# List scatters behind the state decays and two weight splits a step later in attention; expert 2's rows transposed during expert 1's first GEMM

## The chip, the cores and the metric

One NeuronCore of a Trainium2 chip runs the whole program. The metric is the device time of one execution in microseconds, the median of several runs. Five engines work side by side, each through its own instruction stream in order: TensorE (PE, matrix products; its weight loads are PEld), VectorE (DVE), ScalarE (ACT), GpSimd (POOL) and SyncE (SP, which here does nothing but issue transfers). They wait for each other through semaphores. POOL also issues the indirect transfers (gathers and scatters by a list of row numbers).

## The reference

Two stages. The first is linear attention with decay for 4 batches, 8 heads, 768 positions of 64 numbers, in blocks of 64; the second is a mixture of 8 experts of which each of the 3072 tokens takes 2.

```python
# attention, block b of 64 positions
intra = np.einsum('bhic,bhjc->bhij', qb, kb) * Dmask[None]
intra = np.einsum('bhij,bhjd->bhid', intra, vb)
inter = np.einsum('bhid,bhde->bhie', qb * lam_pow[None], kv_state)
out[:, :, sl] = intra + inter
kv_state = lam_block[None, :, None, None] * kv_state + np.einsum('bhsd,bhse->bhde', kb_dec, vb)
...
# experts; x is the attention output, 3072 x 512
noisy_logits = x @ w_gate + np.log1p(np.exp(x @ w_noise)) * noise
top2 = np.argpartition(-noisy_logits, 2, axis=1)[:, :2]        # and softmax of the two
for e in range(E):
    for k in range(2):
        mask = top2[:, k] == e
        h = np.maximum(x[mask] @ w1[e], 0.0)                   # 512 x 1024
        out[mask] += top2_w[mask, k, None] * (h @ w2[e])       # 1024 x 512
```

## The kernel before

**Attention.** Twelve steps t = 0 to 11 of 256 positions each (two chunks of 128, all heads). A step transposes keys and queries of the next step (`trans_k`, `trans_q`), updates the states (`kv`), forms the output (`intra`, `inter`, evacuated by `evac_o` on ACT as `xo`), transposes the output of the step before to tokens (`turn_x`, ACT tile `xc`, stored as `x_tok`) and computes its gate logits. In `kv`, POOL multiplies a state by its decay (line 408, "S") and DVE adds the new product (line 409). The gate's many small DVE instructions are generators that `advance(n)` lets run a few at a time between the steps; `gate`, `route` and `weights` make for each token its two experts, its place in their lists and its weights.

**Lists.** Each chunk of 128 tokens and each of the two choices is one indirect transfer of POOL (`scatter_list`, line 622) that writes 128 records to the lists `lst` in DRAM: 48 of them. `paced(n, tile)` puts a one-element POOL copy in front of n of them, so that they start no earlier than the tile that it reads.

**Weights.** All products of the experts run in three passes with a high and a low part of each fp32 operand. A weight tile is loaded to a staging tile `wst` (four buffers), ACT makes the high part (line 768) and POOL or DVE the low part (line 772). During attention the tables `LOADS`, `HIGH`, `LOW` give the step in which each of expert 0's tiles is loaded and split; `(2, 0)` is the first tile of its second weight.

**Experts.** Expert 0 runs first, then 1, then 2 to 7 in an order by load. A row of an expert is a token; rows come in tiles of 128, at most 7, the last a shorter one. Per expert: gather the rows of `x_tok` (`gather_rows`, POOL, line 810, tile `xg`), transpose them, split into high and low (`xth`, `xtl`), first GEMM (`gemm1`, 8 blocks f of 128 columns, for each of two parts of the rows; ACT and DVE evacuate, lines 863 and 867), second GEMM (`gemm2`, tile by tile; DVE line 907 adds the earlier output, POOL line 914 scatters it). For experts 2 to 7 the transposition goes through DRAM: `turn_rows` transposes 32 x 32 blocks on DVE into a tile `ot` and SP stores it (lines 829 and 831), `fetch_rows` reads it back on SP in four transfers (line 836), `split_rows` makes the two parts on ACT and DVE (lines 843 and 844). The tiles `ot` are three buffers, shared by `turn_rows` and the results of `gemm2`.

For experts 3 to 7, `turn_rows` and `fetch_rows` stand in the second part of the first GEMM of the expert before, and only `split_rows` in its second GEMM. For expert 2 they all stand between the tiles of expert 1's second GEMM (lines 1169 to 1176): after `gemm2(1, t)` the split of weight tile t, the load of the next weight tile, the fetch of row tile t - 1, the turning of row tile t, and the split of row tile t - 1. The last tile (`late`) is split in expert 2's first GEMM. The order is the order of the code: nothing rearranges it.

Of the kernel before, what the change touches and what calls it, by code (L numbers as in the profile page):

```python
# [39 lines left out]
FB = F // 128  # L40
# [21 lines left out]
HIGH = {4: [(1, 0)], 5: [(1, 1)], 6: [(1, 2)], 7: [(1, 3)], 8: [(2, 0)], 9: [(2, 1)]}  # L62
# [21 lines left out]
def size(e, t):  # L84
    return TS if t < NT - 1 else TAILS[e]
# [31 lines left out]
def kernel(  # L117
# [174 lines left out]
    def scatter(n):  # L292
        for job in scatters[:n]:
            scatter_list(*job)
        del scatters[:n]
# [125 lines left out]
    XC = {}  # L421
# [243 lines left out]
    def paced(n, tile):  # L665
        if scatters:
            nc.gpsimd.tensor_copy(spacer, tile[0:1, 0:1])
            scatter(n)
# [265 lines left out]
    for t in range(NST):  # L934
        u = t + 1
        if t:
            products(t - 1)
            turn_x(t - 1)
            paced(1, XC[t - 1][:, 1, 0, :])
# [6 lines left out]
        if u < NST:  # L946
            kv(u)
        kdecay(t + 2)
        scatter(1)
# [8 lines left out]
        paced(1, XO[t][:, 1, 0, :])  # L958
# [12 lines left out]
        if u < NST:  # L971
            if LOW.get(t):
                nc.gpsimd.tensor_copy(spacer, AT[u][0][0:1, 0, 0, 0, 0:1])
            for which, j in LOW.get(t, []):
                split_low(which, 0, j, low=nc.gpsimd)
# [151 lines left out]

    for e in range(1, E):
# [4 lines left out]
        for i, (t0, n) in enumerate(parts(e)):  # L1133
            for f in range(FB):
# [8 lines left out]
                if e == 2 and not i and f == 1:  # L1143
                    split_rows(late, size(2, late))
                    gather_rows(3, late)
# [15 lines left out]
        for t in range(tiles(e)):  # L1161
            gemm2(e, t)
            if e == 1:
                next(ovj, None)
            if e + 1 < E:
                if t < 4:
                    split_w(1, e + 1, t)
                    load_w(2, e + 1, t)
                for j in nxt[t - 1:t] if e == 1 and t else ():
                    fetch_rows(j, size(2, j))  # L1170
                for j in nxt[t:t + 1] if e == 1 else ():
                    turn_rows(j, size(2, j))
                for j in (nxt[t - 1:t] if t else ()) if e == 1 else nxt[t:t + 1]:
                    split_rows(j, size(e + 1, j))
                    if e + 2 < E and j < tiles(e + 2):
                        gather_rows(e + 2, j)
        if e == 1:
            late = nxt[-1]
            fetch_rows(late, size(2, late))
# [62 lines left out]
```

## Time and profile before

| | |
|---|---|
| median of 3 runs (lowest, highest) | 738.89 us (736.31, 739.82) |
| profiled execution, its own time | 741.05 us |
| its span, first to last instruction | 739.3 us |
| busy PE, PEld | 706.7 us (96%), 601.7 us (81%) |
| busy DVE, POOL, ACT | 357.6 us, 274.9 us, 237.0 us |
| mean granted clock of TensorE | 0.989 |

The profile's rows give a start and a duration in microseconds, the engine, the line of the kernel, and for each group what the engine waited for. PE is the engine that is almost always busy, so what matters is where it stands still. "The chain" is the work that ended last, followed back step by step to what released it.

### The profile page before, as it was taken

What the parts mean: (1) busy time and instruction counts of PE and PEld (TensorE: products, weight loads), DVE (VectorE), ACT (ScalarE), POOL (GpSimd) and SP (SyncE); (2) the same over time, 40 slices, a digit from 0 to 9 for tenths busy, and PEclk for the clock granted to TensorE, in tenths of its full rate; (3) what the DMA queues carried; (4) which work ended last, traced back from release to release, by engine and by line L of the source; (5) the groups of instructions that cost most, each with busy time, mean ns of one, the idle gap of its engine ahead of it and who ended that gap; (6) DMA issues with size and microseconds to landing.
All of it is one profiled execution on the core that took longest, in us unless ns stands there. A gap on an engine that the chain in (4) does not pass through costs nothing.

```text
span 739.3 us, 13508 instructions
## 1 busy us (share of the span) xinstructions
PE 706.7 (96%) x4917; PEld 601.7 (81%) x4917; DVE 357.6 (48%) x815; ACT 237.0 (32%) x451; POOL 274.9 (37%) x439
## 2 busy tenths in 40 slices
PE   8899998899999999769999999999999999999996
PEld 6788886699888887658888887988798898889885
DVE  6335869777235543455436433644353544335211
ACT  1567685331133320142214221423042322224200
POOL 3200336677756442323252415242512433221311
PEclk9999999999999999989999999999999999999999
DMA  7999997981527636457464636564655556550211
GB/s 162 204 230 232 245 255 210 272 243 39 114 62 264 185 87 195 141 156 217 147 222 138 178 129 228 158 187 145 208 150 178 193 173 180 161 166 14 79 43 38
DMA packets 139594, 122.50 MB, mean 166 GB/s; under 512 B 88554, under 2 KB 107370, under 8 KB 139524
## 3 DMA queue, kind: packets, MB, share of 16 engines
q1 hardware_dynamic: 124996, 85.22, 43.7%
q0 software_dynamic: 13104, 36.34, 15.6%
q8 instruction: 40, 0.66, 0.4%
q14 instruction: 30, 0.25, 0.1%
q10 hardware_dynamic: 1424, 0.04, 0.1%
HBM read 87.15 MB, written 35.55 MB: 166 GB/s over the span
## 4 chain that ended last, share of the span: by engine, by line
PE 75%; DMA 9%; issue 6%; DVE 4%; ACT 2%; SPq 2%; POOL 1%; POOLq 0%; ACTq 0%; DVEq 0%
PE pS L857 34%; PE pKV L895 14%; PE pO L895 12%; DMA wst<-in_moe_w_dram 3%; DMA xg<-turned 2%; PE pS L356 2%; PE pKV L369 2%; PE pO L369 2%; PE pO L900 1%; PE pS L326 1%; PE pS L429 1%; SPq L836 1%; PE pS L401 1%; POOL out_dram L914 1%; DMA qt<-in_q_dram 1%
## 5 line engine op out<-in xcount | busy, mean ns | idle before, releaser
L857 PE MATMUL pS<-xth,w1h 128*128 128x512 f32 (+3 forms) x544 | 182.0, 335 | 7.7 <-DVE ht L867 5.8
L857 PE MATMUL pS<-xtl,w1h 128*128 128x512 f32 (+3 forms) x544 | 181.3, 333 | 0.4 <-DVE xtl L822 0.4
L857 PE MATMUL pS<-xth,w1l 128*128 128x512 f32 (+3 forms) x544 | 181.1, 333 | 0.0
L863 ACT ACTIVATE ht<-pS 128x512 fp32r<-128x512 f32 (+3 forms) x136 | 65.6, 483 | 218.7 <-PE pS L857 213.0
L867 DVE SCALAR_TENSOR_TENSOR ht<-pS,ht 128x256 fp32r<-128x256 f32 (+3 forms) x176 | 76.5, 455 | 112.1 <-ACT ht L863 110.1
L895 PE MATMUL pO<-w2h,ht 128*128 128x512 f32 x384 | 124.1, 394 | 3.9 <-DVE ot L907 3.9
L895 PE MATMUL pKV<-w2h,ht 128*128 128x512 f32 x384 | 123.0, 391 | 0.0
L857 PEld LDWEIGHTS pS<-xth,w1h 128*128 128x128 f32 x544 | 103.5, 190 | 17.6 <-ACT ht L863 6.0
L857 PEld LDWEIGHTS pS<-xtl,w1h 128*128 128x128 f32 x544 | 103.5, 190 | 9.4 <-DVE xtl L822 0.7
L857 PEld LDWEIGHTS pS<-xth,w1l 128*128 128x128 f32 x544 | 103.5, 190 | 8.9
L914 POOL DMA_INDIRECT out_dram<-ot,rec x46 | 59.2, 1286 | 118.3 <-DVE ot L907 110.3
L895 PEld LDWEIGHTS pO<-w2h,ht 128*128 128x128 f32 x384 | 72.8, 190 | 20.7 <-DVE ot L907 4.3
L895 PEld LDWEIGHTS pKV<-w2h,ht 128*128 128x128 f32 x384 | 72.1, 188 | 16.2
L810 POOL DMA_INDIRECT xg<-x_tok,rec x46 | 49.4, 1074 | 91.3 <-DVE xtl L844 45.5
L895 PE MATMUL pO<-w2l,ht 128*128 128x512 f32 x192 | 76.0, 396 | 0.0
L895 PE MATMUL pKV<-w2l,ht 128*128 128x512 f32 x192 | 75.4, 393 | 0.0
L879 POOL DMA_INDIRECT pv<-out_dram,rec x46 | 47.1, 1023 | 31.7 <-issue 25.2
L843 ACT ACTIVATE xth<-xg 128x512 fp32r<-128x512 f32 (+1 forms) x39 | 22.4, 598 | 105.5 <-DMA xg<-turned 105.5
L622 POOL DMA_INDIRECT lst<-recs,dest x48 | 47.7, 993 | 13.6 <-issue 9.0
L844 DVE TENSOR_TENSOR xtl<-xg,xth 128x512 fp32r<-128x512 f32 (+1 forms) x39 | 25.6, 656 | 46.7 <-ACT xth L843 46.7
L1151 POOL COPY spacer<-ht 1x1 f32<-1x1 f32 x53 | 9.4, 177 | 99.6 <-ACT ht L863 99.5
L907 DVE SCALAR_TENSOR_TENSOR ot<-pKV,rec,pv 128x512 f32<-128x512 f32 x21 | 15.8, 750 | 59.8 <-PE pKV L895 57.1
(228 smaller groups left out, 932.3 us busy)
## 6 DMA issues: line engine op xcount, KB each, us to landing
wst<-in_moe_w_dram SPq DMA_DIRECT2D x48, 512.0 KB, 4.6
turned<-ot SPq DMA_DIRECT2D x36, 256.0 KB, 3.1
xg<-turned SPq DMA_DIRECT2D x144, 64.0 KB, 2.1
wst<-in_moe_w_dram SPq DMA_DIRECT2D x32, 256.0 KB, 4.0
kt<-in_k_dram SPq DMA_DIRECT2D x24, 256.0 KB, 5.2
qt<-in_q_dram SPq DMA_DIRECT2D x24, 256.0 KB, 5.5
vt<-in_v_dram SPq DMA_DIRECT2D x24, 256.0 KB, 5.3
x_tok<-xc SPq DMA_DIRECT2D x12, 512.0 KB, 5.4
```

Source lines behind the costliest of these rows:

```text
L369: nc.tensor.matmul(PO[u][a][half(g), hp, :], lhs, rhs, start=n == 1, stop=n == (8 if u % NW or a else 4))
L622: st = nc.gpsimd.indirect_dma_start(out=lst, out_offset=bass.IndirectOffsetOnAxis(ap=r["dest"][:, i, c:c + 1], axis=0), in_=r["rec"][:, c, ...
L810: nc.gpsimd.indirect_dma_start(out=XG[t][:size(e, t)], out_offset=None, in_=x_tok[:rows, :], in_offset=bass.IndirectOffsetOnAxis(ap=at, ax ...
L843: nc.scalar.activation(hi, p, AF.Copy)
L844: nc.vector.tensor_tensor(lo, p, hi.bitcast(FT), op=SUB)
L857: nc.tensor.matmul(p, W1[a][d][:, fs], xt(b, cs)[:, d], start=(d == 0 and i == 0), stop=(d == DB - 1 and i == 2))
L863: nc.scalar.activation(ht(e, 0, f, cs), p, AF.Relu)
L867: nc.vector.scalar_tensor_tensor(ht(e, 1, f, c), p[:, r], 0.0, ht(e, 0, f, c).bitcast(FT), op0=OP.max, op1=SUB)
L879: nc.gpsimd.indirect_dma_start(out=PV[t][:size(e, t), :], out_offset=None, in_=out, in_offset=bass.IndirectOffsetOnAxis(ap=REC[e, t][:, 0: ...
L895: nc.tensor.matmul(p, ht(e, a, f, cs), W2[b][f // 2][:, f % 2, :], start=(i == 0), stop=(i == len(terms) - 1))
L907: nc.vector.scalar_tensor_tensor(o, p, w, pv, op0=MULT, op1=ADD)
L914: st = nc.gpsimd.indirect_dma_start(out=out, out_offset=bass.IndirectOffsetOnAxis(ap=REC[e, t][:, 0:1], axis=0), in_=o, in_offset=None, bo ...
```

## The change

Four things. In attention, `paced` after `xc` moves from ahead of the key transposes to behind `kv`, the unpaced `scatter(1)` goes, a scatter paced by the scores' tile `at` comes in ahead of the low split, and the last step's `xo` paces two: three list scatters a step as before, in other places. The high splits `(2, 0)` and `(2, 1)` move from steps 8 and 9 to 9 and 10. For expert 2, `turn_next(k)` turns row tile k and fetches row tile k - 2; it stands in the second part of expert 1's first GEMM from block f = 3 on, and then ahead of each `gemm2(1, t)`. The splits are made one place earlier, and `late` is gone.

```diff
--- before.py
+++ after.py
@@ -59,7 +59,7 @@
 FILLA, FILLB, FILLC = {4: 24, 5: 24, 6: 20, 7: 20, 8: 19, 9: 19, NST - 1: 24}, 2, 4
 FILL1, FILL2 = 4, 9
 LOADS = {2: [(1, 0)], 4: [(1, 1)], 5: [(1, 2)], 6: [(1, 3)], 7: [(2, 0)], 8: [(2, 1)], 10: [(2, 2)], 11: [(2, 3)]}
-HIGH = {4: [(1, 0)], 5: [(1, 1)], 6: [(1, 2)], 7: [(1, 3)], 8: [(2, 0)], 9: [(2, 1)]}
+HIGH = {4: [(1, 0)], 5: [(1, 1)], 6: [(1, 2)], 7: [(1, 3)], 9: [(2, 0)], 10: [(2, 1)]}
 LOW = {5: [(1, 0)], 6: [(1, 1)], 7: [(1, 2)], 8: [(1, 3)], 9: [(2, 0)], 10: [(2, 1)]}
 ZEROS = {10: 8, 11: 8}
 MID = 16
@@ -936,7 +936,6 @@
         if t:
             products(t - 1)
             turn_x(t - 1)
-            paced(1, XC[t - 1][:, 1, 0, :])
         if u < NST:
             trans_k(u)
         load(t + 3, "kt")
@@ -945,8 +944,9 @@
         load(t + 3, "qt")
         if u < NST:
             kv(u)
+        if t:
+            paced(1, XC[t - 1][:, 1, 0, :])
         kdecay(t + 2)
-        scatter(1)
         if u == NST:
             logits(t - 1)
         intra(t)
@@ -955,7 +955,7 @@
             store_x(t - 1)
         inter(t, 0)
         evac_o(t)
-        paced(1, XO[t][:, 1, 0, :])
+        paced(1 if u < NST else 2, XO[t][:, 1, 0, :])
         if t and u < NST:
             logits(t - 1)
         if 2 * t in GB[1:]:
@@ -969,8 +969,9 @@
         for which, j in HIGH.get(t, []):
             split_high(which, 0, j)
         if u < NST:
-            if LOW.get(t):
+            if LOW.get(t) and not scatters:
                 nc.gpsimd.tensor_copy(spacer, AT[u][0][0:1, 0, 0, 0, 0:1])
+            paced(1, AT[u][0][:, 0, 0, 0, :])
             for which, j in LOW.get(t, []):
                 split_low(which, 0, j, low=nc.gpsimd)
         advance(FILLA.get(t, 18))
@@ -1125,6 +1126,16 @@
         for i, _ in enumerate(lists(e)):
             load_rec(e, i)
 
+    LAG = 3
+
+    def turn_next(k):
+
+        js = tile_order(2)
+        for j in js[k - 2:k - 1] if k >= 2 else ():
+            fetch_rows(j, size(2, j))
+        for j in js[k:k + 1]:
+            turn_rows(j, size(2, j))
+
     for e in range(1, E):
         if e == E - 1:
             n_over = nc.values_load(ntot[0:1, 0:1], min_val=0, max_val=MAXOV)
@@ -1140,9 +1151,8 @@
                         fetch_rows(f - 1, size(e + 1, f - 1))
                     if f < tiles(e + 1):
                         turn_rows(f, size(e + 1, f))
-                if e == 2 and not i and f == 1:
-                    split_rows(late, size(2, late))
-                    gather_rows(3, late)
+                if e == 1 and i and f >= LAG:
+                    turn_next(f - LAG)
                 if i == 0 and f % 2 == 0:
                     split_w(2, e, f // 2)
                 if i == 0 and f % 2 and e + 1 < E:
@@ -1159,6 +1169,8 @@
             prepare(e + 2)
         nxt = tile_order(e + 1) if e + 1 < E else []
         for t in range(tiles(e)):
+            if e == 1:
+                turn_next(t + FB - LAG)
             gemm2(e, t)
             if e == 1:
                 next(ovj, None)
@@ -1166,17 +1178,10 @@
                 if t < 4:
                     split_w(1, e + 1, t)
                     load_w(2, e + 1, t)
-                for j in nxt[t - 1:t] if e == 1 and t else ():
-                    fetch_rows(j, size(2, j))
-                for j in nxt[t:t + 1] if e == 1 else ():
-                    turn_rows(j, size(2, j))
-                for j in (nxt[t - 1:t] if t else ()) if e == 1 else nxt[t:t + 1]:
+                for j in nxt[t:t + 1]:
                     split_rows(j, size(e + 1, j))
                     if e + 2 < E and j < tiles(e + 2):
                         gather_rows(e + 2, j)
-        if e == 1:
-            late = nxt[-1]
-            fetch_rows(late, size(2, late))
     with tc.For_i(0, n_over) as it:
         e_r = nc.sync.value_load(tab[0:1, 0, bass.ds(it, 1)], min_val=0, max_val=E - 1)
         row = nc.sync.value_load(tab[0:1, 1, bass.ds(it, 1)], min_val=0, max_val=E * STRIDE - OV)
```

The instructions are the same; their places differ. On POOL, around attention step 9: `S` are the state decays, `xc`, `xo` and `at` the tiles that pace, `lst` the lists, `w1l_336` and `w2l_341` low weight parts.

```order
 L772 TENSOR_TENSOR w1l_336<-wst,w1h_332 128x1024
-L667 COPY spacer<-xc 1x1
-L621 MEMSET spacer 1x1
-L622 DMA lst<-recs,dest 29696x2
 L408 TENSOR_TENSOR S_187<-S_186,QS 128x256
 L408 TENSOR_TENSOR S_188<-S_187,QS 128x256
+L667 COPY spacer<-xc 1x1
 L621 MEMSET spacer 1x1
 L622 DMA lst<-recs,dest 29696x2
```

The two decays come first, and the scatter that was ahead of them is behind them. A little further on, at the end of the step:

```order
-L973 COPY spacer<-at 1x1
+L667 COPY spacer<-at 1x1
+L621 MEMSET spacer 1x1
+L622 DMA lst<-recs,dest 29696x2
 L772 TENSOR_TENSOR w2l_341<-wst,w2h_337 128x1024
+L408 TENSOR_TENSOR S_189<-S_188,QS 128x256
```

One scatter now stands between the copy of `at` and the low part, and the next step's decay directly behind the low part.

SP during expert 1's second GEMM, before (`turned_364` to `366` are the stored row tiles 4, 5, 6, `xg` the fetched ones, `wst` weight loads):

```order
L831 DMA turned_364<-ot 128x512
L748 ISA
L748 DMA wst<-in_moe_w_dram 128x2x512
L836 DMA xg_2430<-turned_364 32x4x128 x4
L831 DMA turned_365<-ot 128x512
L748 ISA
L748 DMA wst<-in_moe_w_dram 128x2x512
L836 DMA xg_2432<-turned_365 32x4x128 x4
L831 DMA turned_366<-ot 32x512
```

And after the change, from the end of expert 1's first GEMM on:

```order
L831 DMA turned_364<-ot 128x512
L831 DMA turned_365<-ot 128x512
L836 DMA xg_2430<-turned_364 32x4x128 x4
L831 DMA turned_366<-ot 32x512
L836 DMA xg_2432<-turned_365 32x4x128 x4
L831 DMA turned_360<-ot 128x512
L836 DMA xg_2434<-turned_366 32x128 x4
L831 DMA turned_361<-ot 128x512
L733 TENSOR_LOAD order
```

Three fetches and five stores now precede the record loads of expert 3 (the group that begins with `order`), and the first weight load comes one more fetch and store after those.

DVE at the start of expert 1's second GEMM, before (`xg_2430` is row tile 4, `w1l` the low weight parts, `ot<-pKV` and `ot<-pO` the evacuation of a tile):

```order
L907 SCALAR_TENSOR_TENSOR ot<-pKV,rec_3186,pv_2424 128x512
L1102 TENSOR_TENSOR ovg<-ovg,tail 1x320
L772 TENSOR_TENSOR w1l_333<-wst,w1h_329 128x1024
L829 STREAM_TRANSPOSE ot<-xg_2430 128x512
L907 SCALAR_TENSOR_TENSOR ot<-pO,rec_3186,pv_2425 128x512
L1104 TENSOR_REDUCE ovt<-ovg 1x40
L772 TENSOR_TENSOR w1l_334<-wst,w1h_330 128x1024
L829 STREAM_TRANSPOSE ot<-xg_2432 128x512
L844 TENSOR_TENSOR xtl_348<-xg_2430,xth_346 128x4x128
```

And after:

```order
L829 STREAM_TRANSPOSE ot<-xg_350 128x512
L829 STREAM_TRANSPOSE ot<-xg_2426 128x512
L907 SCALAR_TENSOR_TENSOR ot<-pKV,rec_3186,pv_2424 128x512
L1103 TENSOR_TENSOR ovg<-ovg,tail 1x320
L772 TENSOR_TENSOR w1l_333<-wst,w1h_329 128x1024
L844 TENSOR_TENSOR xtl_348<-xg_2430,xth_346 128x4x128
L829 STREAM_TRANSPOSE ot<-xg_2428 128x512
L907 SCALAR_TENSOR_TENSOR ot<-pO,rec_3186,pv_2425 128x512
```

The first row tile is split one tile sooner, six of the seven transposes are done before the first evacuation, and the seventh before the second.

## Rows read from the trace of the kernel before

**Rows 1.** Busy time by stretch: length, busy us per engine, clock, DMA share.
```profile
267.00:304.00 37.00, 33.08 (x138) 26.66 (x137) 13.71 (x21) 5.49 (x7) 10.23 (x11) 0.95 0.47 140
304.00:324.00 20.00, 12.56 (x74) 11.03 (x73) 8.77 (x20) 4.45 (x8) 7.03 (x10) 0.91 0.51 160
```

**Rows 2.** Chain that ended last: start, duration, work.
```profile
267.03 5.52 PE pKV L895 x24
...
355.37 5.49 PE pO L895 x24
...
388.33 3.65 PE pO L900 x16
391.98 34.45 PE pS L857 x192
```

**Rows 3.** Timeline of PE, expert 1 to 2, rows after a standstill (in brackets).
```profile
298.43 0.50 PE L895 MATMUL pO<-w2h,ht 128*128 128x512 f32 x1 [3.92 <-DVE ot L907]
...
323.49 0.58 PE L857 MATMUL pS<-xth,w1h 128*128 128x288 f32 x1 [5.79 <-DVE ht L867]
```

**Rows 4.** The chain in expert 1's second GEMM, one tile.
```profile
290.01 0.41 SPq L748
...
291.97 4.21 DMA xg<-turned
296.36 0.64 ACT xth L843
...
299.93 0.41 SPq L748
```

**Rows 5.** Timelines of ACT, POOL, SP and DVE near expert 1's second GEMM.
```profile
260.08 0.44 ACT L863 ACTIVATE ht<-pS 128x320 fp32r<-128x320 f32 x1 [1.32 <-PE pS L857]
...
266.65 1.03 POOL L810 DMA_INDIRECT xg<-x_tok,rec  x1 [0.54 <-issue]
...
280.91 1.87 SPq L836 DMA_DIRECT2D xg<-turned  x4
...
274.78 0.69 DVE L829 STREAM_TRANSPOSE ot<-xg 128x512 f32<-128x512 f32 x1
```

**Rows 6.** Transfers from 250 to 330 us: size, median us to landing.
```profile
turned<-ot SPq DMA_DIRECT2D x6, 256.0 KB, 3.5
...
xg<-x_tok,rec POOLq DMA_INDIRECT x14, 3.5
```

**Rows 7.** Timeline of DVE, last turning in expert 3's first GEMM.
```profile
428.39 0.70 DVE L829 STREAM_TRANSPOSE ot<-xg 32x512 f32<-32x512 f32 x1 [3.26 <-DMA turned<-ot]
```

**Rows 8.** Timeline of PE in attention steps 9 to 11.
```profile
116.70 1.14 PE L326 MATMUL pS<-identf,qt 128*128 128x128 f32 x8 [1.78 <-ACT xc L430]
...
129.15 1.15 PE L326 MATMUL pS<-identf,qt 128*128 128x128 f32 x8 [1.30 <-ACT xc L430]
...
139.80 0.59 PE L447 MATMUL pL<-sel,xp 128*128 128x16 f32 x4 [1.19 <-DVE pos L566]
```

**Rows 9.** Timeline of ACT, the two high splits.
```profile
114.84 1.06 ACT L768 ACTIVATE w2h<-wst 128x1024 fp32r<-128x1024 f32 x1 [4.31 <-DMA wst<-in_moe_w_dram]
...
127.28 1.06 ACT L768 ACTIVATE w2h<-wst 128x1024 fp32r<-128x1024 f32 x1 [4.85 <-DMA wst<-in_moe_w_dram]
```

**Rows 10.** Timeline of DVE, two long gate instructions.
```profile
113.98 2.08 DVE L465 SCALAR_TENSOR_TENSOR ga<-zc 128x64 f32<-128x64 f32 x1
...
138.35 1.10 DVE L564 TENSOR_SCALAR past<-past,base 128x8 f32<-128x8 f32 x1
```

**Rows 11.** Busy time: PE, PEld, DVE, ACT, POOL in attention steps 8 to 10.
```profile
111.00:129.00 18.00, 14.82 (x204) 11.73 (x201) 17.21 (x65) 9.32 (x22) 12.06 (x18) 1.00 0.78 214
```

**Rows 12.** Timeline of POOL: two low parts, a gather of expert 0.
```profile
113.62 2.34 POOL L772 TENSOR_TENSOR w1l<-wst,w1h 128x1024 fp32r<-128x1024 f32 x1
...
137.07 2.35 POOL L772 TENSOR_TENSOR w2l<-wst,w2h 128x1024 fp32r<-128x1024 f32 x1
...
176.39 1.04 POOL L810 DMA_INDIRECT xg<-x_tok,idx  x1 [1.63 <-DVE found L593]
```

## The prediction, written before the changed kernel ran

> **What bounds the kernel now.** I read the page's shares first: PE is busy 706.7 of 739.3 us, so the sum of its standstills is some 33 us, and the question for every edit is which standstill it shortens. The table of busy time by stretch says where they lie. In the stretch from 267 to 304 us PE is busy 33.1 of 37 us and in the one from 304 to 324 only 12.6 of 20, at a mean granted clock of 0.95 and 0.91 of full speed [rows 1]; expert 3's first GEMM, by contrast, is one piece of the chain, 192 matmuls without a gap [rows 2]. So the turn from expert 1 to expert 2 is the one large hole behind attention.
>
> The chain gives its size. Expert 1's second GEMM starts at 267.03, and expert 2's second GEMM at 355.37 [rows 2]. Between them lie expert 1's second GEMM (six whole tiles and a short one) and expert 2's first. Where PE is never late these take 5.49 us a whole tile, 3.65 us the short one and 34.45 us the first GEMM of expert 3, which has the same tiles as expert 2 [rows 2]. That is 6 x 5.49 + 3.65 + 34.45 = 71.0 us, against 355.37 - 267.03 = 88.3. The hole is 17.3 us. The timeline shows it only in part, as waits for DVE before one evacuation (3.92 us) and one within expert 2's first GEMM (5.79 us) [rows 3]; the rest is matmuls at the lower granted clock of rows 1 and shorter waits.
>
> The chain inside the hole is a loop over SP [rows 4]. SP issues a weight load at 290.01, behind it the fetch of a row tile; the fetch lands 4.21 us after its last issue; ACT splits it (0.64 us at 296.36); DVE, in order, makes the row's low part, evacuates the next tile and makes the low part of the next weight tile; that frees a staging buffer, and SP can issue the next weight load, at 299.93. One turn takes 9.9 us where PE needs 5.49. The loop closes because the fetch that a tile's split needs stands in SP's queue behind a weight load that waits for DVE, and DVE's next evacuation stands behind that split.
>
> **Expert 2's rows, one layer sooner.** Removed from the loop: the four fetch issues and their landing. Nothing is added: seven turnings on DVE, seven stores and 28 fetch issues on SP, moved. What each needs:
>
> - Gathers. The last of the seven is issued at 266.65, one for each block of 0.44 + 1.32 = 1.76 us [rows 5], so the first at about 256.1; with 3.5 us to landing [rows 6] gather k lands at 259.6 + 1.76 k. Turning k stands behind the evacuation of block k + 3; block 3's starts at 260.08 on ACT [rows 5], and DVE is through with it about 1 us later: 261.1 + 1.76 k. It is ready, with 1.5 us to spare.
> - DVE. Turnings of 0.69 us [rows 5] join five blocks of 1.76 us. DVE's other work there is an evacuation and small table instructions; I estimate each at about a turning, 1.0 to 1.4 us a block together, so DVE falls behind by at most 0.3 us a block, 1.5 us in all. PE sees it only if the low part of the last block is late: the second GEMM needs that in the last three of its first tile's 24 matmuls, 7/8 x 5.52 = 4.8 us after 267.03. Hidden.
> - SP. Store 0 issues at about 261.8 and lands 3.5 us later [rows 6], at 265.3; its fetch takes 1.87 us to issue [rows 5] and at most the 4.2 us of rows 4 to land: 271.4. The split of row tile 0 stands behind the first evacuation and the first weight split, at 267.03 + 5.52 + about 2 = 274.5. Tile 0 is 3 us early. Fetches run two tiles behind turnings, so SP's round is between 1.87 + 0.4 = 2.3 us (issues alone) and half of 3.5 + 1.87 + 0.4, 2.9 us; PE consumes a tile each 5.49 us. The lead grows. The last two fetches still stand behind weight loads, of t = 1 and 2, which wait for DVE's split of those; the second is free at about 267 + 3 x 5.5 + 2 = 285.5, its row tile is wanted at about 304. Not late.
> - Expert 3's record loads now queue behind three fetches, at about 272 to 275 instead of ahead of everything. Behind them on POOL waits the first gather of expert 3, and behind that the second scatter, wanted at 278 or so. At worst some us on POOL, which no matmul waits for until the three `ot` buffers are all held.
> - Those three buffers are the new risk. Turnings and evacuations share them, and a turning waits until the store of three tiles ago has landed. The trace shows such a wait at its worst in expert 3's first GEMM: 3.26 us [rows 7]. Here turning 5 and the first evacuation stand behind stores 2 and 3, at 270 and about 273; the first evacuation is due at 272.6 and PE needs its bank back only two tiles after the start, at 278.0. Between 0 and the 8 us of the crowded case below, I take 1.0 us, nearer to the free end, since tile 2 has 5 us of slack.
>
> So -17.3 + 1.0 = -16.3 us. What is late next: nothing in this stretch; PE goes on as in expert 3.
>
> **Attention.** In steps 8 and 9 ACT waits 4.31 and 4.85 us for the loads of expert 0's second weight [rows 9], with `xc` behind it, and PE waits 1.78 and 1.30 us for `xc` [rows 8]. A step later the loads have landed (ACT got them at 114.84 and 127.28), and the splits cost 1.06 us of ACT each, beside PE's work. The most to be had is 1.78 + 1.30 + the 1.19 us that PE waits for DVE at 139.80 [rows 8], 4.3 us.
>
> But DVE is busy 17.2 of the 18 us from 111 to 129 [rows 11], so PE would soon wait for DVE: the 0.8 us of DVE's idle time is the nearest row. And DVE is held by POOL: a gate instruction of 128 x 64 lasted until 116.06 while a low part ran on POOL from 113.62 to 115.96, and one of 128 x 8 until 139.45, with a low part from 137.07 to 139.42 [rows 10, 12]. PE's wait at 139.80 rests on the second. With the scatter paced by `at` ahead of it, each low part starts one indirect issue (1.04 us in rows 12) and its pacing later, and the decays, which come sooner, no longer hold DVE's state additions. A hold can fall on another instruction and last up to the 2.35 us of a low part. Bounds: -4.3 to +2.4; I take -1.0.
>
> The Trainium skill ("SBUF — State Buffer", Who interferes with whom) says that a DVE instruction with two SBUF inputs, or in a mode that uses both ports, and a GpSimd instruction exclude each other for the whole instruction, and that issue order decides who waits. The two long rows agree. By a rule of no interference the attention term would be -3.1, by this one it depends on where the low parts fall.
>
> The list scatters stay three a step, so POOL has as many left at the end of attention. Their later chain has slack: POOL waits 1.63 us for DVE at 176.39 [rows 12], so up to 1.6 us of an earlier end passes on to the experts; more would wait there.
>
> **The sum.** -16.3 - 1.0 = -17.3 us. On the profiled execution's own 741.05 us that is 723.8. That execution lies 2.2 us above the median of the runs, which is what the change is measured against: 738.89 - 17.3 = 721.6 us.
>
> **The rivals.**
>
> - Crowded transfers. The hole's two stretches moved 140 GB/s x 37 us + 160 x 20 = 8.4 MB [rows 1]. In 36.6 us that would be 229 GB/s; attention shows 214 [rows 11]. If the stretch reaches halfway between 160 and 214, 187 GB/s, it takes 44.9 us, and 8.3 us of the gain are lost: 738.9 - 17.3 + 8.3 = 730. For it: the fetch took 4.2 us to land even at 140 GB/s. Against: the lead of the fetches, and weight tiles that are wanted only after 304.
> - Attention loses. Expert 2's turn comes in full, and a low part's hold falls where PE needs DVE: 738.9 - 16.3 + 2.4 = 725. For it: rows 10. Against: the decays no longer wait behind scatters.
> - Slower, by the ring. Turnings block DVE, in order, on stores, and the evacuations with it. If each of the seven tiles waits w us, PE loses 7 w less its two tiles' slack of 11 us. At the measured 3.26 us it is 11.8 us, a gain still; it eats the gain from w = (17.3 + 11) / 7 = 4.0 us on, and at 5 us it loses 24 - 17.3 = 6.7 us: 746. For it: rows 7. Against: that wait came where fetches ran one tile behind turnings; here they run two behind.
> - The loop stays. Some fetch is still behind a weight load that waits for the evacuation it feeds: 739. SP's new order speaks against it.
>
> **How the numbers follow.** Full gain 0.70, crowded transfers 0.15, attention loses 0.09, slower by the ring 0.04, the loop stays 0.02. The likeliest gives 721.6. The range goes down by what attention may give beyond my value, 3.3 us, and a run below the median, to 717.5, and up to the crowded case, 730. The measurement of this kernel tells some 0.5%, 3.7 us, from no change. Faster by more than that are the first three, 0.94; within it the last, 0.02; slower 0.04.
>
> **What would show it.** In the changed profile: ACT's waits for fetched row tiles in expert 1's second GEMM gone (they are the loop); PE busy in all of 267 to 338 at a granted clock of 1.00; expert 2's second GEMM starting 71 us after expert 1's; DVE waits for `turned` stores of up to 3 us, none followed by PE. In attention: no ACT wait for a weight load in steps 8 and 9, PE's waits of 1.78 and 1.30 us gone, and new ones for DVE in their place. I am wrong if PE waits for DVE's evacuation within expert 1's second GEMM, or if the first fetch lands after 275.

## The result, and the profile after

The changed kernel takes 725.78 us (median of 4 runs, 724.48 to 726.85), against 739.34 us for the kernel before (4 runs): a ratio of 0.983, 95% interval 0.981 to 0.985. The forecast was 721.6, in a range from 717.5 to 730. The profiled execution is the shortest of the four, 724.48 us with a span of 722.6; that of before, 741.05, lay above its median. The profiled pair thus differs by 16.6 us, the medians by 13.6.

The two stretches of [rows 1], in the kernel after, by the same view (the fields after the length: PE, PEld, DVE, ACT, POOL, clock, DMA share, GB/s):

```profile
267.00:304.00 37.00, 36.12 (x158) 29.33 (x157) 17.15 (x29) 7.23 (x10) 19.32 (x19) 1.00 0.68 212
304.00:324.00 20.00, 20.00 (x130) 18.69 (x129) 13.29 (x30) 9.40 (x16) 3.98 (x8) 1.00 0.57 161
```

PE is busy 56.1 of 57 us where it was busy 45.6, and the granted clock is 1.00 in both. The transfers of the first stretch went up from 140 to 212 GB/s, and PE was not held by them.

The chain of the kernel after through the same place, as in [rows 2]:

```profile
279.91 8.47 DMA out_dram<-ot,rec
...
289.31 5.79 PE pKV L895 x24
295.09 5.49 PE pO L895 x24
300.59 3.66 PE pKV L900 x16
304.25 34.45 PE pS L857 x192
338.69 5.49 PE pO L895 x24
```

The loop over SP of [rows 4] is gone from it. One wait is left, and the timeline of PE, where expert 1's second GEMM starts at 266.27, shows its size:

```profile
266.27 0.40 PE L895 MATMUL pKV<-w2h,ht 128*128 128x512 f32 x1
...
289.31 0.51 PE L895 MATMUL pKV<-w2h,ht 128*128 128x512 f32 x1 [0.88 <-DVE ot L907]
```

From 266.27 to 338.69 it is 72.4 us, against the 88.3 of before and the 71.0 without any standstill. The 0.88 us comes from the ring of three `ot` buffers (e7 below takes one user out of the ring, and the waits of the evacuations for a scatter go). The timeline of DVE:

```profile
271.01 0.71 DVE L829 STREAM_TRANSPOSE ot<-xg 128x512 f32<-128x512 f32 x1 [2.46 <-DMA turned<-ot]
...
278.88 0.75 DVE L907 SCALAR_TENSOR_TENSOR ot<-pO,rec,pv 128x512 f32<-128x512 f32 x1 [2.53 <-DMA out_dram<-ot,rec]
...
288.50 0.75 DVE L907 SCALAR_TENSOR_TENSOR ot<-pKV,rec,pv 128x512 f32<-128x512 f32 x1 [6.76 <-PE pO L895]
```

The evacuation at 288.50 is put down to PE, but PE had been done with that bank; the chain shows the scatter of the tile before it, which took 8.47 us and ended at 288.38. ACT's rows:

```profile
119.51 1.05 ACT L768 ACTIVATE w2h<-wst 128x1024 fp32r<-128x1024 f32 x1
133.78 1.06 ACT L768 ACTIVATE w2h<-wst 128x1024 fp32r<-128x1024 f32 x1
...
270.47 0.63 ACT L843 ACTIVATE xth<-xg 128x512 fp32r<-128x512 f32 x1 [2.56 <-DMA xg<-turned]
...
280.29 0.63 ACT L843 ACTIVATE xth<-xg 128x512 fp32r<-128x512 f32 x1 [4.94 <-DMA xg<-turned]
```

The two high splits no longer wait for their loads [rows 9]. ACT still waits for fetched row tiles, up to 4.94 us, but PE no longer waits behind it.

In attention the waits for `xc` [rows 8] are gone, and these stand in their place on PE:

```profile
120.20 2.08 PE L356 MATMUL pS<-qT,kT 64*128 64x128 f32 x30 [1.45 <-DVE qTs L333]
...
129.65 0.19 PE L532 MATMUL pL<-ob,lstrict 128*128 128x64 bf16 x1 [2.02 <-DVE ob L498]
...
139.96 0.59 PE L447 MATMUL pL<-sel,xp 128*128 128x16 f32 x4 [2.53 <-DVE pos L566]
```

That is 6.00 us, where the three waits of [rows 8] made 4.27. On DVE three gate instructions of the kernel after are long, two of them those of [rows 10]:

```profile
112.00 2.95 DVE L465 SCALAR_TENSOR_TENSOR ga<-zc 128x64 f32<-128x64 f32 x1
...
127.03 1.63 DVE L492 CAST ei<-mi 128x16 f32<-128x16 uint32 x1
...
137.15 2.45 DVE L564 TENSOR_SCALAR past<-past,base 128x8 f32<-128x8 f32 x1
```

And POOL, with its low parts [rows 12] and what stands ahead of the last:

```profile
112.48 2.37 POOL L772 TENSOR_TENSOR w1l<-wst,w1h 128x1024 fp32r<-128x1024 f32 x1
...
126.25 2.36 POOL L772 TENSOR_TENSOR w2l<-wst,w2h 128x1024 fp32r<-128x1024 f32 x1
...
135.72 0.18 POOL L667 COPY spacer<-at 1x1 f32<-1x1 f32 x1
...
136.20 0.99 POOL L622 DMA_INDIRECT lst<-recs,dest  x1 [0.16 <-issue]
137.22 2.35 POOL L772 TENSOR_TENSOR w2l<-wst,w2h 128x1024 fp32r<-128x1024 f32 x1
```

Each of the three DVE instructions ends 0.03 to 0.10 us after a low part: 114.95 and 114.85, 128.66 and 128.61, 139.60 and 139.57. They last as long as the low part lets them. Two of the three records start before the low part does, at 112.00 and 137.15, and both starts lie within the list scatter that POOL issues right ahead of it (111.47 to 112.45 in the same view, and 136.20 to 137.19): the first instruction is held for 2.95 us, longer than a low part. Two more instructions are longer, beside the state decay that now follows the low part: line 99 takes 0.51 us at 114.98 and line 495 takes 0.65 at 128.69 (0.20 and 0.29 in the kernel before).

### The profile page after: what moved, and what is told of

It is laid out like the page before. It is cut to its first block, busy times and chain, and to the rows that moved or that the text cites. A ratio compares the mean times of both kernels' runs of the same rounds, so it can differ in the third digit from the quotient of the medians.

```text
span 722.6 us, 13511 instructions
## 1 busy us (share of the span) xinstructions
PE 702.7 (97%) x4917; PEld 599.8 (83%) x4917; DVE 361.2 (50%) x815; ACT 238.5 (33%) x451; POOL 279.4 (39%) x439
## 4 chain that ended last, share of the span: by engine, by line
PE 82%; DVE 6%; issue 5%; DMA 4%; SPq 2%; POOL 1%; ACT 1%; POOLq 0%; ACTq 0%; DVEq 0%
PE pS L857 36%; PE pKV L895 15%; PE pO L895 14%; PE pS L356 3%; PE pKV L369 2%; PE pO L369 2%; PE pO L900 2%; PE pS L429 1%; DMA out_dram<-ot,rec 1%; DVE at L359 1%; PE pKV L900 1%; PE pS L313 1%; PE pS L326 1%; POOL out_dram L914 1%; PE pS L819 1%
## 5 line engine op out<-in xcount | busy, mean ns | idle before, releaser
L914 POOL DMA_INDIRECT out_dram<-ot,rec x46 | 61.1, 1329 | 124.5 <-DVE ot L907 107.0
L907 DVE SCALAR_TENSOR_TENSOR ot<-pO,rec,pv 128x512 f32<-128x512 f32 x21 | 15.8, 750 | 60.4 <-PE pO L895 57.9
```

The source lines that it names most:

```text
L907: nc.vector.scalar_tensor_tensor(o, p, w, pv, op0=MULT, op1=ADD)
L914: st = nc.gpsimd.indirect_dma_start(out=out, out_offset=bass.IndirectOffsetOnAxis(ap=REC[e, t][:, 0:1], axis=0), in_=o, in_offset=None, bo ...
```

## The experiments

All were timed in five rounds beside the kernel before, in three sets of four, each set on one chip. The last four columns are from each profile: the sum of the three DVE instructions of lines 465, 492 and 564; attention, from PE's first gate product (line 417) to its last; from there to expert 1's first GEMM; and the stretches of 4 us within attention, by their start, in which the granted clock was under 0.9. The kernel before had medians of 745.26 us beside the first set, 738.34 beside the second and 743.20 beside the third.

| kernel | median us | ratio to before, 95% | three DVE us | attention us | to expert 1 us | clock under 0.9 |
|---|---|---|---|---|---|---|
| before | 739.34 | 1 | 3.36 | 113.2 | 86.8 | none |
| after | 725.78 | 0.983 (0.981 to 0.985) | 7.03 | 113.4 | 86.0 | none |
| e1 expert 2 only | 729.68 | 0.979 (0.976 to 0.982) | 3.35 | 113.1 | 91.1 | 120, 124 |
| e2 attention only | 750.05 | 1.007 (1.004 to 1.009) | 7.01 | 115.0 | 92.7 | 120, 124, 140, 144 |
| e3 after again | 731.57 | 0.981 (0.978 to 0.984) | 7.05 | 113.4 | 93.3 | none |
| e4 low parts in four | 730.97 | 0.982 (0.979 to 0.985) | 1.74 | 111.8 | 95.2 | none |
| e5 later splits | 721.39 | 0.977 (0.975 to 0.979) | 3.37 | 112.4 | 86.0 | 120, 124 |
| e6 scatters only | 727.87 | 0.985 (0.982 to 0.988) | 7.01 | 115.9 | 87.8 | 140, 144, 148 |
| e7 seventh aside | 721.78 | 0.978 (0.976 to 0.980) | 3.37 | 112.5 | 86.0 | 120, 124 |
| e8 expert 2, in four | 722.60 | 0.978 (0.977 to 0.980) | 3.87 | 113.5 | 86.0 | 140 |
| e9 low part ahead | 728.09 | 0.979 (0.975 to 0.984) | 2.89 | 109.7 | 95.1 | none |
| e10 after, third time | 732.75 | 0.985 (0.982 to 0.989) | 7.01 | 115.0 | 90.9 | 120, 124, 140, 144 |
| e11 later splits again | 727.53 | 0.978 (0.974 to 0.982) | 3.36 | 112.4 | 90.9 | 120, 124 |
| e12 later, in four | 727.32 | 0.978 (0.975 to 0.981) | 3.95 | 111.9 | 92.8 | 136, 140 |

The stretch to expert 1 is 86 to 88 us in the first measurement and the second set, and over 90 in the other two, whatever the kernel; so times are compared within a set. The clock column matters as much for the lengths of attention. The code of attention is the same in before, e1 and e7: 113.2 us without a fall of the clock, 113.1 and 112.5 with one from 120 us on, so a fall there costs nothing that shows. A fall in the last step does: after, e3 and e10 are one kernel, and its last step (from its gate products to the next) takes 8.5 us in the first two and 10.1 in e10.

**e1, e2: the two halves apart.** e1 is the changed kernel with `HIGH` and the attention loop of before; e2 the changed `HIGH` and attention loop with the expert loops of before.

```diff
 # e1, against the changed kernel
-HIGH = {..., 9: [(2, 0)], 10: [(2, 1)]}
+HIGH = {..., 8: [(2, 0)], 9: [(2, 1)]}
...
+            paced(1, XC[t - 1][:, 1, 0, :])     # ahead of trans_k again
...
-        if t:
-            paced(1, XC[t - 1][:, 1, 0, :])
...
+        scatter(1)
...
-        paced(1 if u < NST else 2, XO[t][:, 1, 0, :])
+        paced(1, XO[t][:, 1, 0, :])
...
-            if LOW.get(t) and not scatters:
+            if LOW.get(t):
...
-            paced(1, AT[u][0][:, 0, 0, 0, :])
```

> Only the earlier turning of expert 2's rows; attention as before. Theory A (the whole gain is the loop at expert 2): the stretch from expert 1's second GEMM to expert 2's second GEMM falls from 88.3 to about 72 us as in the changed kernel, and the time is that of the changed kernel within 0.3%, 724 to 728 us. Rival B (the attention edits bring part of the timed 13.6 us): the stretch falls the same, but the time stays 3 us or more above the changed kernel's, 729 or more.

> Only the moved list scatters and high splits; expert 2 as before. Theory A: within 1.5 us of the kernel before, 737 to 741 us; PE's waits for xc are replaced by waits for DVE (about 1.4, 2.0 and 2.5 us). Rival B: 3 us or more faster than before, 736 or less.

Measured: e1 0.979, 15.6 us less than before; e2 1.007, 4.8 us more. The times in the expectations were those of the first chip, and on this one the kernel before takes 745.26, so the ratios count. By them the expert 2 edit brings at least what the whole change brings (0.981 in e3, on the same chip; the intervals overlap), and the attention edits alone cost, which neither expectation had. The three DVE instructions in e1, by the timeline:

```profile
114.56 2.08 DVE L465 SCALAR_TENSOR_TENSOR ga<-zc 128x64 f32<-128x64 f32 x1
...
129.30 0.18 DVE L492 CAST ei<-mi 128x16 f32<-128x16 uint32 x1
...
139.24 1.09 DVE L564 TENSOR_SCALAR past<-past,base 128x8 f32<-128x8 f32 x1
```

Together 3.35 us, 3.7 us less than after the change, with the same operands.

**e3, e4: the changed kernel again, and its low parts cut in four.**

```diff
-                split_low(which, 0, j, low=nc.gpsimd)
+                for qt_ in range(4):          # 256 columns each
+                    split_low(which, 0, j, qt_, low=nc.gpsimd, n=4)
```

> The changed kernel once more, unaltered, on the same chip as the others: 724 to 727 us. If its profile is of a slower execution than the first one's 724.5 us, the stretches show where executions of one program differ: theory A expects attention and expert 1 to 2 to agree within 0.5 us, and the difference in the granted clock at the start or the end.

> The changed kernel with each low part that POOL makes in attention cut into four instructions of 256 columns. Theory C (POOL's long instruction holds DVE's next one until it ends, and that is what took the attention gain): the three DVE instructions of 2.9, 1.6 and 2.5 us fall below 0.9 us each, PE's waits of 2.0 and 2.5 us for DVE fall by 1 us or more each, and the time falls by 1.5 to 3 us against the changed kernel. Rival D (DVE is simply full of gate work there): PE's waits stay within 0.5 us and the time within 1 us. Rival E (the four pieces keep the hold between them, or POOL's extra instructions cost more): the same or up to 1 us slower.

Measured: 0.981 and 0.982, not to be told apart. e3 differs from the first profile of the same kernel in the stretch to expert 1 (93.3 for 86.0 us), not in attention. The three instructions shrink in e4 (7.0 to 1.74 us), but the holds are partly handed on: lines 99 to 105, the next four behind line 465, take 0.62 to 0.73 us each there, and about 0.2 in the kernel before. Attention is 1.5 us shorter than in e3, at a clock of 1.00 in both, and the next stretch 1.9 us longer. Of that 1.7 lie between the first gather of expert 1 and its GEMM (20.1 for 18.4 us), where PE waits 1.73 us at 236.97 for a low part of the rows. What attention gains is given back, and the time does not fall as theory C had it.

**e5, e6: the two attention edits apart**, each with the expert 2 edit. e5 is e1 with the changed `HIGH`; e6 is the changed kernel with the `HIGH` of before.

```diff
 # e5, against e1; e6 is the reverse line against the changed kernel
-HIGH = {..., 8: [(2, 0)], 9: [(2, 1)]}
+HIGH = {..., 9: [(2, 0)], 10: [(2, 1)]}
```

> The expert 2 edit and, of the attention edits, only the two high weight splits a step later; the list scatters stand where they stood before. Known so far, all against the kernel before on one chip: the expert 2 edit alone 0.979, the whole change 0.981, the attention edits alone 1.007. Theory F (the scatters' new places are what costs; the later splits help): PE's waits of 1.78 and 1.30 us for xc go and nothing takes their place, so it is 0.976 or below, that is 2 us or more under the expert 2 edit alone. Rival G (the later splits only let PE run on until DVE is late, so that they bring nothing): 0.979, with PE waits for DVE (qTs, ob or pos) of 1.5 to 2.5 us in steps 9 to 11 as in the changed kernel. Rival H (the later splits are what costs, since the low parts on POOL start behind them and so later): 0.981 or above, as the whole change.

> The whole change but for the two high splits, which stay in steps 8 and 9: the expert 2 edit and the list scatters in their new places. Theory F (the scatters' places cost): 0.982 to 0.985, worse than the expert 2 edit alone (0.979) by 2 us or more, with PE's waits for xc (about 1.8 and 1.3 us) still there and the low parts of POOL holding DVE at later instructions. Rival G (each of the two is worth nothing by itself): 0.979. Rival H (the later splits cost): 0.979 or below.

Measured: e5 0.977, e6 0.985, 6.5 us apart, as theory F had e6. The scatters' places cost: e6 is 6.1 us above e7, which differs from e6 in them and in the ring edit below, worth nothing that shows. The later splits by themselves are worth nothing that can be told (e5 against e7, which has the splits of before, 0.4 us). PE's waits in e5:

```profile
122.37 3.47 PE L356 MATMUL pS<-qT,kT 64*128 64x128 f32 x30 [1.87 <-DVE qTs L333]
...
139.45 0.59 PE L447 MATMUL pL<-sel,xp 128*128 128x16 f32 x4 [1.18 <-DVE pos L566]
```

Without the `xc` waits PE waits for DVE at line 356, as rival G has it, but the wait for `pos` is 1.18 us as before. In e6 that wait is 2.53 us again, and what follows shows in its busy time by stretch (clock third from the end):

```profile
138.00:142.00 4.00, 1.68 (x12) 1.67 (x14) 3.76 (x10) 0.48 (x1) 3.13 (x4) 0.74 0.80 189
142.00:146.00 4.00, 4.00 (x44) 3.27 (x40) 1.85 (x13) 0.00 (x0) 0.00 (x0) 0.50 0.97 364
146.00:150.00 4.00, 2.75 (x16) 1.95 (x17) 0.00 (x0) 2.06 (x4) 2.00 (x5) 0.50 0.74 262
```

After the standstill the granted clock is 0.50, the 1.2 GHz level. In e5 it stays at the 2.4 GHz level here; its own fall lies earlier, behind the wait at line 356, whose thirty products took 3.47 us (2.08 in the changed kernel), and is over by then:

```profile
124.00:128.00 4.00, 4.00 (x48) 3.19 (x47) 3.90 (x18) 0.59 (x2) 3.65 (x6) 0.73 0.53 202
...
138.00:142.00 4.00, 2.82 (x43) 2.41 (x45) 3.66 (x14) 0.95 (x2) 3.31 (x6) 1.00 1.19 276
142.00:146.00 4.00, 2.55 (x36) 1.79 (x34) 1.54 (x9) 2.43 (x5) 1.84 (x6) 1.00 0.95 332
```

The last step, from its gate products to the next, takes 7.18 us in e5 and 11.12 in e6: 1.35 from the longer wait, and the other 2.6 fall in the stretch at the lower clock.

**e7: the ring.** e1 with the seventh turning written to a constant tile that is idle by then.

```diff
-            turn_rows(j, size(2, j))
+            turn_rows(j, size(2, j), zero if k in (6,) else None)
```

> The expert 2 edit alone, with the seventh turning written to a tile that lies idle then instead of one of the three shared buffers, so that the first evacuations of expert 1's second GEMM no longer wait for a store or for the scatter of the tile just before. In the changed kernel PE lost 0.51 us there, at 289.31, and no more. If the ring of buffers costs what this wait shows, the time is 0 to 0.9 us below the expert 2 edit alone: 0.978 to 0.979, not to be told from it. If the ring costs more than is seen (it also delays the scatters and so the gathers of expert 3), 0.976 or below.

Measured: 0.978, as e1 and e5. The ring is what held the evacuations: that of the third tile waits for a scatter in e5 and for PE, as it should, in e7. DVE in e5:

```profile
286.67 0.75 DVE L907 SCALAR_TENSOR_TENSOR ot<-pKV,rec,pv 128x512 f32<-128x512 f32 x1 [5.83 <-DMA out_dram<-ot,rec]
```

And in e7:

```profile
281.59 0.75 DVE L907 SCALAR_TENSOR_TENSOR ot<-pKV,rec,pv 128x512 f32<-128x512 f32 x1 [2.63 <-PE pKV L895]
```

But there is nothing to win: in e5, with the ring as it is, PE does not stand still here at all. Its chain, from expert 1's first GEMM to expert 2's:

```profile
229.85 36.06 PE pS L857 x192
...
265.91 5.51 PE pKV L895 x24
...
302.55 34.41 PE pS L857 x192
```

From 265.91 to the end of that first GEMM, 336.96, it is 71.05 us.

**e8: e1 with the low parts in four.** The edit of e4.

> The expert 2 edit alone, and the low weight parts that POOL makes in attention cut into four instructions of 256 columns each. In the whole change the same cut made attention 1.5 us shorter and expert 0 longer by as much. Theory C (a long POOL instruction holds DVE for its length, and the hold reaches PE): attention is again about 1.5 us shorter than with the expert 2 edit alone; and as the list scatters here stand earlier on POOL, less is given back in expert 0: 0.976 to 0.978. Rival D (POOL has no slack behind attention, so whatever attention gains is waited for at expert 1's rows): attention shorter, the whole time as with the expert 2 edit alone, 0.979 to 0.980. Rival E (PE waits for DVE's own work, not for POOL's hold): nothing shorter anywhere.

Measured: 0.978, as e7 on the same chip. The three DVE instructions take 3.87 us, no less than with long low parts (3.37 in e7), and attention is not shorter in this profile. Theory C is not refuted by that, for its last step ran at a lower clock than e7's (0.60 from 140 to 144) and took 9.23 us for 7.17; the three steps before it were 1.0 us shorter than in e7 (34.2 for 35.2). That the length of an early low part does not matter to the time is what the medians say (722.60 and 721.78); why is not shown.

**e9: the low part ahead of the scatter.** The changed kernel with one pair swapped.

```diff
-            if LOW.get(t) and not scatters:
+            if LOW.get(t):
                 nc.gpsimd.tensor_copy(spacer, AT[u][0][0:1, 0, 0, 0, 0:1])
-            paced(1, AT[u][0][:, 0, 0, 0, :])
             for which, j in LOW.get(t, []):
                 split_low(which, 0, j, low=nc.gpsimd)
+            paced(1, AT[u][0][:, 0, 0, 0, :])
```

> The whole change with one pair of places swapped: in each step the low weight part stands ahead of the scatter paced by the scores' tile, not behind it, so that it starts about 1.2 us sooner; the decays keep their new place ahead of the other scatters. Theory J (the scatter in front of the low part is the whole cost: it moves the part's hold of DVE onto the instructions that PE waits for, the 128x16 cast and the 128x8 addition): the addition at the last low part is back from 2.45 us to about 1.1, PE's wait for pos from 2.53 to about 1.2, and the ratio to before comes to that of the kernel with only the later splits, 0.977 (against about 0.981 to 0.983 for the whole change). Rival K (the other places cost: fewer scatters are done by the end of attention, or the decays in front make POOL late elsewhere): the waits go but the ratio stays at 0.980 or above, with the loss behind attention.

> The changed kernel unaltered, to stand beside the others on this chip: 0.981 to 0.983 of before by its two earlier measurements.

> The expert 2 edit and only the later high splits, a second time, beside the changed kernel on the same chip: 0.977 of before if its first measurement holds, that is some 3 to 4 us under the changed kernel. If the scatters' places cost nothing and the chips differed, it is level with the changed kernel.

Measured on one chip: e9 728.09 us, the changed kernel (e10) 732.75, the later splits without the scatters' places (e11) 727.53. Only the place of the scatter before the low part (and one more one-element copy of 0.18 us) separates e9 from e10, and e9's median is 4.7 us less; the intervals of the ratios still overlap (to 0.984, from 0.982), while those of e10 and e11 just do not. The trace is plainer. DVE in e9:

```profile
108.81 2.48 DVE L359 TENSOR_TENSOR at<-pS,Mk 128x512 f32<-128x512 f32 x4 [0.75 <-PE pS L356]
111.21 1.43 DVE L465 SCALAR_TENSOR_TENSOR ga<-zc 128x64 f32<-128x64 f32 x1
...
113.41 0.61 DVE L107 TENSOR_SCALAR gacc<-gu 128x64 f32<-128x64 f32 x1
...
125.31 0.27 DVE L492 CAST ei<-mi 128x16 f32<-128x16 uint32 x1
...
133.78 1.19 DVE L564 TENSOR_SCALAR past<-past,base 128x8 f32<-128x8 f32 x1
```

And POOL in e9:

```profile
110.19 2.37 POOL L772 TENSOR_TENSOR w1l<-wst,w1h 128x1024 fp32r<-128x1024 f32 x1
...
112.99 1.00 POOL L622 DMA_INDIRECT lst<-recs,dest  x1 [0.16 <-issue]
...
132.44 0.18 POOL L973 COPY spacer<-at 1x1 f32<-1x1 f32 x1
132.59 2.35 POOL L772 TENSOR_TENSOR w2l<-wst,w2h 128x1024 fp32r<-128x1024 f32 x1
```

The low part starts 0.15 us after the copy of `at` starts, not 1.50 (135.72 and 137.22 in the kernel after), and 1.1 us of it lie beside the scores' product of line 359, which is 2.48 us long whether a low part runs with it or not (2.48 at 109.60 in the changed kernel, where none does). The gate instructions are back to 2.89 us, and PE's wait for `pos` is 1.27. Attention is 109.7 us. That is 5.3 less than in e10, whose clock fell twice, and 3.7 less than in the first profile of the changed kernel and in e3, whose clock, like that of e9, did not fall: 3.7 us is what the place of this scatter costs in attention. It is also 3.5 us less than in the kernel before, so the other attention edits, with the low part ahead, do shorten attention; which of them does it no run separates.

The rows at 113.41 and 112.99 show that a scatter's issue holds DVE too: line 107 ends 0.03 us after the issue, and takes 0.61 us where it takes 0.20 in the kernel before. The same is in e5 and e12 (0.60 and 0.61).

But the stretch behind attention is 95.1 us in e9, 4.2 more than in e10. Rival K is right in that the loss lies there, but not in its cause: the last list scatter comes 67.1 us behind attention, as in e10 (67.3) and e11 (66.5). What is longer is the time from the first gather of expert 1 to its GEMM, 21.4 us for 17.1 in e10. PE in e9:

```profile
218.34 0.66 PE L819 MATMUL pS<-identf,xg 128*128 128x128 f32 x4 [0.77 <-DMA xg<-x_tok,rec]
...
230.43 0.38 PE L819 MATMUL pS<-identf,xg 128*128 128x128 f32 x2 [0.71 <-issue]
...
234.12 0.69 PE L819 MATMUL pS<-identf,xg 64*128 64x64 f32 x4 [3.32 <-DVE xtl L822]
```

PE stands still at expert 1's rows. The profiled execution, 731.84 us, is one of the longer ones of e9; its six runs spread from 725.04 to 734.40. What held DVE and ACT until 230.45 in it, the trace does not name, and it stays open. e10 itself came at 0.985 where 0.981 to 0.983 had been expected, and e11 at the 0.978 of its first measurement (0.977).

**e12: the later splits, and low parts in four.** e5 with the edit of e4.

> The expert 2 edit, the later high splits, the list scatters where they stood before, and POOL's low parts in four instructions of 256 columns. If a hold by POOL is what makes PE wait for DVE in steps 9 to 11 of the kernel with the later splits (1.87 us for qTs), each hold is at most a quarter as long, attention is 1 to 2 us shorter and the ratio 0.975 to 0.976. If four instructions give DVE's other instructions as many short holds as one long one, the same 0.977; the trace then has long DVE instructions at other lines.

Measured: 0.978, as e11. Of the time the second of the two expectations came. Attention is 0.5 us shorter, the stretch behind it 1.9 longer. Here too the last step ran at a lower clock (0.71 and 0.50 from 136 to 144) and took 8.78 us for 7.40; the three before it were 2.0 us shorter than in e11 (32.9 for 34.9), which is what the first expectation had for attention.

The version that beats both kernels is the change without its scatter edits (e5). On one chip it takes 727.53 us (e11) where the changed kernel takes 732.75 (e10). e7 and e8, which also leave the splits where they were, cannot be told from it.

## Why the prediction was right, and where it was wrong

The large term came as it was reasoned, and the small one did not. That the time still fell within the range owes something to luck: the upper end, 730, was set for the crowded transfers, which did not come.

**Expert 2's turn: right.** Forecast -17.3 + 1.0; the trace gives 72.4 us for 88.3, -15.9, and e1 alone -15.6. The loop over SP was the hole: with the fetches ahead of the weight loads it is gone, and the granted clock is 1.00. The 1.0 us for the ring was 0.88 here, nothing in e5 and 1.31 in e9. The text said that it would be wrong if PE waited for DVE's evacuation in this GEMM; PE does, once, for the 0.88. The ring wait came from a scatter of 8.47 us, not from a `turned` store, which the step had named, and it came at the third tile, whose 5 us of slack were the step's reason for a small value; that the size fits is partly luck. ACT's waits for fetched tiles were to be gone; they are there, off the path.

**Crowded transfers: did not come.** The first 37 us moved 212 GB/s, and all 57 us 194 (212 x 37 + 161 x 20, over 57), more than the 187 of the rival, with PE busy in 98% of them. The rival's 229 GB/s set the bytes of 57 us against the 36.6 us of the second GEMM alone; against 57 less the 17.3 of the hole it would have been 211.

**Attention: wrong in sign, by the medians.** Forecast -1.0 between -4.3 and +2.4. The attention edits cost 4.8 us alone (e2) and 1.9 beside the expert 2 edit on the same chip (e3 less e1, within the noise); the scatter edits by themselves cost 5.2 (e10 less e11). On the first chip, -13.6 less the expert 2 term of -16 leaves about +2. The profiled execution there, the fastest of its four, shows none of it: attention 113.4 us for 113.2, the stretch behind it 86.0 for 86.8. The rival that came is "attention loses", at 725.

The step that failed is the sentence on the scatter ahead of the low part, "each low part starts one indirect issue (1.04 us in rows 12) and its pacing later". It was told as a neutral shift. But the rows of before already say what a shift does: the held instruction ended at 116.06 with the low part at 115.96, and at 139.45 with 139.42 [rows 10, 12]. A held instruction ends when the low part ends, so a low part that starts later holds DVE longer by as much, up to its whole length. Behind the copy of `at` the low part starts 1.35 us later (1.50 us against 0.15). Three of them would make 4.1 us on DVE, which was busy 17.2 of 18 us [rows 11]; the sum of the three instructions is 3.7 us longer, 7.03 against 3.36, and attention 3.7 us longer than with the low part ahead (e3 against e9). The term was to be had from the rows: 3 x (1.04 + pacing), above zero, set against the 4.3 us of gain. The upper bound took one hold of at most a low part's 2.35 us; there were three, and one lasted 2.95, for the scatter's issue ahead of the low part holds DVE as well.

So in attention at an even clock the gain (3.5 us in e9) and the holds (3.7) cancel. What the medians show beyond that is in part the clock below, in part the stretch to expert 1 (e3 against e1, 2.2 us), and for the latter the cause stays open.

Here the rule weighed in the forecast holds. By the Trainium skill ("SBUF — State Buffer", Who interferes with whom) an instruction of DVE with at most one SBUF input and outside the two-port modes does not contend with GpSimd; a cast and a scalar operation can. The scores' product reads PSUM and one SBUF tile and takes 2.48 us with and without a low part beside it, and the cast of 128 x 16 takes 0.18 without and 1.63 with one. The trace agrees.

**The upper bound was too low** for some executions. In e6, e2 and e10 a wait of 2.53 us is followed by a granted clock of 0.50 to 0.57 and a last step 1.6 to 2.6 us longer still; in the first profile of the changed kernel and in e3 the same wait leaves the clock at 1.00. The bounds counted the holds and not the clock behind them.

**The later splits** remove PE's waits for `xc`, as forecast, and bring nothing, since DVE is late in their place (1.87 us in e5). This was the forecast's own remark on DVE's 0.8 us of idle time, and it held.

**The slack behind attention** was put at 1.6 us. e4, e9 and e12 make attention 1.5, 5.3 and 0.5 us shorter and lose 1.9, 4.2 and 1.9 in the next stretch. In e4 and e9 the list scatters did pass the gain on, and it was lost behind expert 1's first gather.

## What to carry to other kernels

When an instruction of POOL that holds DVE is moved, look at when it ends, since the held instruction ends with it: ask which DVE instruction stands beside it then, and put it beside one that reads PSUM. A fetch that stands in a queue behind a load which waits for the work that the fetch feeds closes a loop; issue the fetches ahead of those loads, and the hole goes as a whole. Test the small edit of a change apart from the large one: here the large one hid that the small one cost. And set the lengths of a stretch beside each other only where the granted clock agrees.

## What the runs showed of the hardware

A POOL product of 128 x 1024 (2.35 us) made a DVE instruction of 128 x 8 last 2.45 us (1.09 where it came later beside the low part, in e1), and DVE was free 0.03 to 0.10 us after POOL. The issue of an indirect transfer by POOL held DVE too: a scalar operation of 128 x 64 took 0.61 us and ended 0.03 us after the issue (114.02 and 113.99 in e9), where it takes 0.20 alone. Four products of 256 columns held the three instructions 1.74 us together where one long one had held them 7.03, but held the four behind the first of them 0.62 to 0.73 us each.

The length of one standstill did not decide whether the granted clock fell. The changed kernel kept 1.00 behind 2.53 us in one profile and had 0.57 over 142 to 146 behind the same wait in another (e10); e2 fell from 1.00 behind 0.84 us (121.77), and the changed kernel did not behind 1.45 (120.20). And the same kernel before took 738.3 to 745.3 us by the chip.
